# A third weight buffer, a later second transform and piecewise adds in a fused attention and mixing kernel

## The chip, the cores and the metric

The kernel runs on one core of one Trainium2 chip. The metric is the device time of one execution in microseconds (us). The profiler also records the span, the time from the first to the last instruction of the execution; the device time is a little longer.

## What is computed

Three blocks follow each other, for 2 batches of 768 tokens:

```python
# attention: 8 heads of 64, each token sees 4 sink keys and a window of 128 keys
a = softmax(where(is_sink | in_window, q @ k.T / 8, -1e9)); x = a @ v        # (2, 768, 512)
# token mixing
theta = x @ w_theta
y = w_tok_r @ (x * cos(theta)) + w_tok_i @ (x * sin(theta))
u = x + y
x = u + relu(u @ w_ch)
# Fourier mixing and a wide layer
u = x + real(fft(fft(x, axis=1), axis=2))
un = (u - mean(u)) / sqrt(var(u) + 1e-6)
out = u + relu(un @ w_ch1) @ w_ch2        # 512 -> 2048 -> 512
```

The weights arrive as 64-bit floats and are turned into 32-bit floats on the chip.

## The kernel before

**Numbers.** A matmul operand is split into a high part and the rest (`split`: a copy on ScalarE, ACT, makes the high part, a subtraction on GpSimd, POOL, or on VectorE, DVE, makes the rest), and each product is three matmuls on TensorE, PE.

**Weights.** A weight tile of 128 x 512 comes from memory as 128 x 1024 words of 32 bits into a raw buffer (`fetch`, one DMA of 512 KB on SP's queue). `conv` makes a 32-bit tile of it: ACT scales the high words into a slot `hs` (L268), DVE shifts them into `t` (L271), ors in bits of the low words (L272), puts the sign on (L275) and so writes the result `w`. Then the raw buffer is free for the next DMA. `ahead(depth)` keeps up to DEPTH transfers under way, `pump(reserve)` converts the oldest one if enough slots are free. There are 58 tiles, in this order: 4 of `w_theta`, 18 of the token weights, 4 of `w_ch`, then 16 pairs of `w_ch1` and `w_ch2`. After the attention the raw buffers are called rawb; a trace names all those loads after one tensor, `in_w_ch_dram`. `t` lies in PSUM (`self.room`) in the token mixing of batch 0 and in chunk 0, otherwise it is `w` itself.

**Slots.** Nearly all tiles are places of 128 x 512 words, handed out by `_Slots` (`take`, `give`).

**Stages.** (1) Attention and theta, to about 170 us of the span. (2) `y_gen(0)`, the token mixing of batch 0: PE accumulates in four banks `p0` (named acc and bank) and two banks `pc`, and at the end six additions on DVE put them onto the transposed activations xT (L812, L815). (3) `y_gen(1)`, the same for batch 1, and between its matmuls the channel mixing and Fourier transform of batch 0 (`chain(0)`: `ch_gen` in 6 steps, then `dft_gen` in 20). (4) The wide layer (`mlp_gen`) in four chunks of 384 rows, each of 16 steps f of 12 matmuls into `pc` and 9 into three of the banks. Chunks 0 and 1 work on batch 0, chunks 2 and 3 on batch 1. The steps of `chain(1)`, the transform of batch 1, are put between the steps f of the wide layer, and in chunk 0 what is left of the weights is fetched and converted. For each f, `jit_split` splits the two weight tiles anew, one step ahead, on ACT (L194) and POOL (L200).

In the transform, `groups` adds and splits spectra (DVE, ACT, POOL), PE multiplies them into two tiles s of 128 x 258 and 128 x 256, ACT copies one of them to a mirror buffer `bs` (L966), GpSimd clears column 0 of `bs` (L967), and DVE makes Y of both.

The calls stand in program order, but a scheduler that works with a timeline of its own decides the final order on each engine; each engine then runs its list strictly in order.

Of the kernel before, what the change touches and what calls it, by code (L numbers as in the profile page):

```python
# [11 lines left out]
F32 = mybir.dt.float32  # L12
F32R = mybir.dt.float32r
I32 = mybir.dt.int32
AF = mybir.ActivationFunctionType
ALU = mybir.AluOpType
# [12 lines left out]
TILES = [(0, False), (3, False), (1, False), (1, True), (2, False), (2, True)]  # L29
GROUPS = [0, 3, 1, 2]  # L30
NSLOT = 67
NSLOT2 = 15
T0 = 2
DEPTH = 2
NRAW = 2
NRAW1 = 3
NJIT = 12
IL = 1
# [2 lines left out]
C1E = 12  # L41
# [29 lines left out]
C1N = 2  # L71
# [55 lines left out]
class _Slots:  # L127
# [5 lines left out]
    def grow(self, pool, n):  # L133
        self.free.extend((pool, f"s{i}") for i in range(n))

    def take(self, *shape, dt=F32, name="t"):
        place = self.free.popleft()
        t = place[0].tile([128, *shape], dt, tag=place[1], name=name, bufs=1)
        if place in self.last:
            self.pairs.append((self.last[place], t))  # L140
        self.last[place] = t
        self.own[id(t)] = (place, t, self.free)
        return t
# [35 lines left out]
class _Body:  # L179
# [76 lines left out]
    def conv(self, tile_):  # L256

        nc = self.nc
        raw = tile_.bitcast(I32)
        w = self.take(512)  # L260

        t = (self.room.next() if self.room else w).bitcast(I32)
        hs = self.take(512)
        v = raw.rearrange("p (n w) -> p n w", w=2)
        lo, hi = v[:, :, 0], v[:, :, 1]


        nc.scalar.activation(  # L268
            hs, raw.bitcast(F32).rearrange("p (n w) -> p n w", w=2)[:, :, 1], AF.Copy, scale=2.0 ** -112
        )  # L270
        nc.vector.tensor_scalar(t, hs.bitcast(I32), 3, None, op0=ALU.logical_shift_left)  # L271
        nc.vector.scalar_tensor_tensor(  # L272
            t, in0=lo, scalar=29, in1=t, op0=ALU.logical_shift_right, op1=ALU.bitwise_or
        )
        nc.vector.scalar_tensor_tensor(  # L275
            w.bitcast(I32), in0=hi, scalar=-0x80000000, in1=t, op0=ALU.bitwise_and, op1=ALU.bitwise_or
        )
        self.give(hs)
        self.raw.append(tile_)
        return w, w  # L280

# [490 lines left out]

    def y_gen(self, b):
        nc = self.nc
        p0 = [self.ps_acc.next() for _ in range(4)]
        pc = [self.ps_pc.next().rearrange("p (a m) -> p a m", a=2) for _ in range(2)]
        for j in range(NS):
            zz = self.z.pop((b, j))
            ws = [self.weight_split("tok", j, c) for c in (0, 2, 1)]
            for c, z in enumerate(zz):  # L780
                zh, zl = self.split(z, "a", "vp"[b], s=self.sz)
                self.give(z)
                (wh, wl), (ch, cl) = ws[2 * c], ws[1]
                cs = slice(256 * c, 256 * c + 256)
                first, last = j == 0 and c == 0, j == NS - 1 and c == 1
                def big(dd):
                    ds_ = slice(dd * 128, (dd + 1) * 128)
                    self.mm(p0[dd], zh[:, ds_], wh, first, False)
                    self.mm(p0[dd], zh[:, ds_], wl, False, False)
                    self.mm(p0[dd], zl[:, ds_], wh, False, last)  # L790

                def small(dd):
                    ds_ = slice(dd * 128, (dd + 1) * 128)
                    q = pc[dd // 2][:, dd % 2]
                    self.mm(q, zh[:, ds_], ch[:, cs], first and dd % 2 == 0, False)
                    self.mm(q, zh[:, ds_], cl[:, cs], False, False)
                    self.mm(q, zl[:, ds_], ch[:, cs], False, last)

                for dd in range(4):
                    big(dd)  # L800
                    small(dd)
                    if dd % 2:
                        if dd == 3:
                            self.give(zh, zl)
                            if c and b:
                                for k in range(3):
                                    self.give(*self.ws.pop(("tok", j, k)))
                        yield
        xt = self.xT[b]
        for dd in range(4):  # L810
            o = xt[:, dd, 0:512]
            nc.vector.tensor_tensor(o, p0[dd], o, op=ALU.add)  # L812
        for g in range(2):
            o = xt[:, 2 * g:2 * g + 2, 512:768]
            nc.vector.tensor_tensor(o, pc[g], o, op=ALU.add)  # L815


    def ch_gen(self, b, ring):
# [51 lines left out]
    def dft_gen(self, b, ring):  # L870
        nc = self.nc
        xt = self.xT[b]
        X = {}
        sums, difs = {}, {}
        for c in range(3):
            lo_, hi_ = xt[:, 0:2, 256 * c:256 * c + 256], xt[:, 2:4, 256 * c:256 * c + 256]
            e, o = self.take(2, 256), self.take(2, 256)
# [72 lines left out]
        for gi, r in enumerate(GROUPS):  # L950
# [4 lines left out]
            n = len(G[r])  # L955
# [8 lines left out]
                self.give(*hl)  # L964
            bs = self.bs.next()[:, 0:256]
            nc.scalar.activation(bs[:, 1:256], pb[:, 1:256], AF.Copy)  # L966
            nc.gpsimd.memset(bs[:, 0:1], 0.0)  # L967
            Y = self.Y.next()
            av = pa[:, 0:256].rearrange("p (r m) -> p m r", m=64)
            bv = bs.rearrange("p (r m) -> p m r", m=64)  # L970
# [25 lines left out]
                yield  # L996
        if b:
            self.give(*self.sd, *self.co, self.ce)

    def norm_tile(self, n):  # L1000
        nc = self.nc
# [97 lines left out]
    def all(self, banded):  # L1099
# [17 lines left out]
        with ExitStack() as ctx:  # L1117
            e = ctx.enter_context(tc.tile_pool(name="e2", bufs=1, reuse_waits="tile"))
            ps = ctx.enter_context(tc.tile_pool(name="ps", bufs=1, space=PSUM, reuse_waits="tile"))
            self.ps_acc = _Ring(ps, 3, [128, 512], F32, "acc", [self.bank])  # L1120
            self.ps_pc = _Ring(ps, 2, [128, 512], F32, "pc")
            self.ps_s = _Ring(ps, 2, [128, 512], F32, "s")
            self.bs = _Ring(e, 2, [128, 256], F32, "bs")
            self.Y = _Ring(e, 2, [128, 514], F32, "Y")
            self.raw = deque(e.tile([128, 1024], F32, name=f"rawb{k}") for k in range(NRAW))
            self.room = self.ps_s
            for _ in range(len(self.fetched)):
                key, raw = self.fetched.popleft()
                self.w[key] = self.conv(raw)
            self.raw = deque(list(self.raw)[0:NRAW])  # L1130
            self.s.grow(e, NSLOT2)
            self.rest()
# [5 lines left out]
    def rest(self):  # L1138
# [45 lines left out]
        for ch in range(4):  # L1184
            mg = self.mlp_gen(ch)
            for f in range(16):
                next(mg)
                if ch == 0 and f >= P2F:
                    self.pump(P2R)
                for _ in range(C1N if ch == 0 and f < C1E else 1):  # L1190
                    next(fill, None)
                if ch == 0 and f >= P2F:
                    self.pump(P2R)
                g = f - NRM[ch]
                if ch < 3 and g in (0, 2, 4):
                    self.norm_tile(3 * ch + 3 + g // 2)
                if ch < 3 and g in (2, 4, 6):
                    self.turn_norm(3 * ch + 3 + (g - 2) // 2, self.ps_s)
                if ch == 0:
                    self.mark(L2)  # L1200
            next(mg, None)
# [95 lines left out]
```

## Time and profile before

| | us |
|---|---|
| median of 3 runs | 656.09 |
| lowest and highest of them | 654.64, 656.84 |
| the profiled execution | 649.25 |
| its span | 647.4 |
| TensorE busy in it | 610.5 |
| granted TensorE clock, mean | 0.969 |

The profile was taken of one execution. A row gives the source line (L275), the engine, the operation and `out<-in` with buffer numbers left out. TensorE's busy time counts matmuls from issue to end, so that it holds short bubbles as well; what a stretch lacks in busy time is idle for certain. PEclk is the granted share of TensorE's clock: 1.00 is 2.4 GHz, half of it 1.2 GHz.

### The profile page before, as it was taken

The numbers are of one execution on the slowest core, as the hardware profiler recorded it, in microseconds if no ns is written. First come the engines' busy times: TensorE is split into PE (matmuls) and PEld (weight loads), VectorE is DVE, ScalarE is ACT, GpSimd is POOL, SyncE is SP. The second block draws the span as 40 slices with busy tenths as digits, with TensorE's granted clock in tenths as the row PEclk, the third lists the DMA queues.
The fourth block names the chain that finished last, engine by engine and source line by source line (L and its number), as shares of the span: only waits on it lengthen the run. The fifth ranks groups of instructions, "written<-read, shape, count | busy, mean of one in ns | idle before, by whom it ended". The sixth has DMA issues, their size and how long they took to land.

```text
span 647.4 us, 9463 instructions
## 1 busy us (share of the span) xinstructions
PE 610.5 (94%) x3446; PEld 524.2 (81%) x3446; DVE 351.8 (54%) x747; ACT 334.3 (52%) x776; POOL 296.1 (46%) x258
## 2 busy tenths in 40 slices
PE   8999999999999699977899987989999999999996
PEld 5767778778788499866699976978999999999995
DVE  5875748656588778697878874664211211121112
ACT  4667667777676542355543553667433444344331
POOL 1221112332584632413653568256566666565561
PEclk8589999999999989999999998999999999999999
DMA  7862423100023534503334410121000100010001
GB/s 247 302 192 82 132 66 89 43 0 2 20 95 93 161 97 132 162 33 98 98 98 131 137 60 1 32 67 50 0 1 0 51 2 0 1 50 0 1 2 55
DMA packets 23337, 46.61 MB, mean 72 GB/s; under 512 B 2512, under 2 KB 9552, under 8 KB 23280
## 3 DMA queue, kind: packets, MB, share of 16 engines
q1 hardware_dynamic: 22032, 43.74, 21.2%
q0 software_dynamic: 1248, 2.17, 1.3%
q8 instruction: 29, 0.48, 0.3%
q14 instruction: 28, 0.23, 0.1%
HBM read 42.75 MB, written 3.15 MB: 71 GB/s over the span
## 4 chain that ended last, share of the span: by engine, by line
PE 66%; DVE 13%; ACT 7%; DMA 7%; issue 4%; POOL 1%; SPq 0%; DVEq 0%; ACTq 0%
PE pc L210 21%; PE acc L210 16%; PE bank L210 6%; PE oa L210 5%; PE s L210 5%; PE th L210 5%; PE tp L215 4%; DMA rawb<-in_w_ch_dram 4%; PE sc L210 4%; DVE t L275 2%; ACT t L194 2%; DVE t L272 2%; DVE t L200 1%; DMA raw<-in_w_tok_iT_dram 1%; ACT t L268 1%
## 5 line engine op out<-in xcount | busy, mean ns | idle before, releaser
L200 POOL TENSOR_TENSOR t<-t 128x512 fp32r<-128x512 f32 x175 | 231.9, 1343 | 210.9 <-ACT t L194 188.5
L210 PE MATMUL pc<-t 128*128 128x384 f32 (+1 forms) x1056 | 199.8, 328 | 1.1 <-ACT t L194 0.6
L210 PEld LDWEIGHTS pc<-t 128*128 128x128 f32 x1056 | 183.9, 192 | 13.3 <-ACT t L194 1.2
L210 PE MATMUL acc<-t 128*128 128x512 f32 x648 | 180.8, 397 | 1.0 <-DVE xT L812 1.0
L194 ACT ACTIVATE t<-t 128x512 fp32r<-128x512 f32 x196 | 116.3, 625 | 94.5 <-PE acc L210 37.3
L210 PEld LDWEIGHTS acc<-t 128*128 128x128 f32 x648 | 117.3, 189 | 19.8 <-DVE xT L812 1.6
L1071 DVE SCALAR_TENSOR_TENSOR t<-pc,t 128x384 fp32r<-128x384 f32 x64 | 35.5, 555 | 150.9 <-ACT t L1070 150.8
L210 PE MATMUL bank<-t 128*128 128x512 f32 x216 | 68.2, 406 | 7.9 <-DVE xT L812 4.2
L210 PE MATMUL s<-t 128*128 128x256 f32 (+2 forms) x480 | 63.1, 283 | 10.7 <-POOL t L200 3.4
L210 PEld LDWEIGHTS s<-t 128*128 128x128 f32 x480 | 60.4, 189 | 14.4 <-POOL t L200 3.6
L1070 ACT ACTIVATE t<-pc 128x384 fp32r<-128x384 f32 x64 | 31.3, 489 | 70.8 <-PE pc L210 65.1
L268 ACT ACTIVATE t<-rawb 128x512 f32<-128x512 f32 x42 | 27.9, 672 | 54.8 <-DMA rawb<-in_w_ch_dram 45.5
L210 PEld LDWEIGHTS oa<-t 128*128 128x128 f32 x352 | 51.2, 209 | 2.5 <-issue 0.7
L210 PE MATMUL oa<-t 128*128 128x64 f32 x352 | 51.9, 276 | 0.0
L210 PEld LDWEIGHTS bank<-t 128*128 128x128 f32 x216 | 38.6, 189 | 16.4 <-ACT t L194 4.6
L746 POOL TENSOR_TENSOR t<-t 128x512 f32<-128x512 f32 x12 | 16.5, 1374 | 72.6 <-DVE t L745 35.1
L493 ACT ACTIVATE p<-sc,nb 128x272 f32<-128x272 f32 (+1 forms) x72 | 33.8, 472 | 18.8 <-DVE nb L489 18.7
L210 PE MATMUL th<-t 128*128 128x512 f32 x144 | 41.9, 417 | 1.5 <-DVE t L200 1.0
L215 PE MATMUL tp<-ident,p 128*128 128x128 f32 x176 | 39.6, 299 | 2.5 <-ACT p L493 2.2
L489 DVE CUSTOM_DVE_ANT_0 sc<-sc,m 128x272 f32<-128x272 f32 (+1 forms) x72 | 29.9, 429 | 18.2 <-PE sc L210 9.7
L210 PE MATMUL sc<-kst,t 64*128 64x272 f32 (+2 forms) x132 | 36.9, 466 | 0.0
L215 PEld LDWEIGHTS tp<-ident,p 128*128 128x128 f32 x176 | 27.0, 171 | 11.7 <-ACT p L493 3.7
(129 smaller groups left out, 683.5 us busy)
## 6 DMA issues: line engine op xcount, KB each, us to landing
rawb<-in_w_ch_dram SPq DMA_DIRECT2D x36, 512.0 KB, 3.6
kst<-in_k_dram SPq DMA_DIRECT2D x12, 256.0 KB, 3.4
t<-in_v_dram SPq DMA_DIRECT2D x12, 256.0 KB, 4.3
out_dram<-t SPq DMA_DIRECT2D x12, 256.0 KB, 2.1
t<-in_q_dram SPq DMA_DIRECT2D x11, 256.0 KB, 3.7
raw<-in_w_theta_dram SPq DMA_DIRECT2D x4, 512.0 KB, 6.4
raw<-in_w_tok_rT_dram SPq DMA_DIRECT2D x4, 512.0 KB, 3.8
raw<-in_w_tok_iT_dram SPq DMA_DIRECT2D x4, 512.0 KB, 4.3
```

The source lines that it names most:

```text
L194: nc.scalar.activation(o, i, AF.Copy)
L200: e.tensor_tensor(o, x, hi.bitcast(F32), op=ALU.subtract)
L210: i = self.nc.tensor.matmul(o, lhsT=lhsT, rhs=rhs, start=start, stop=stop, skip_group_check=True).ins
L215: self.chained(self.nc.tensor.transpose(o, x, ident).ins)
L268: nc.scalar.activation(hs, raw.bitcast(F32).rearrange("p (n w) -> p n w", w=2)[:, :, 1], AF.Copy, scale=2.0 ** -112)
L272: nc.vector.scalar_tensor_tensor(t, in0=lo, scalar=29, in1=t, op0=ALU.logical_shift_right, op1=ALU.bitwise_or)
L275: nc.vector.scalar_tensor_tensor(w.bitcast(I32), in0=hi, scalar=-0x80000000, in1=t, op0=ALU.bitwise_and, op1=ALU.bitwise_or)
L489: nc.vector.tensor_tensor_reduce(out=sc[:, 0:wd], in0=sc[:, 0:wd], in1=mask, op0=ALU.add, op1=ALU.min, scale=-0.125, scalar=3.0e38, accum_ ...
L493: self.last_exp = nc.scalar.activation(p[:, h, 0:wd], sc[:, 0:wd], AF.Exp, bias=nb[:, h:h + 1], scale=-1.0, accum_out=sm[:, h:h + 1]).ins
L746: nc.gpsimd.tensor_tensor(ph, km, ph, op=ALU.subtract)
L1070: nc.scalar.activation(hh, hp, AF.Relu)
L1071: nc.vector.scalar_tensor_tensor(hl, in0=hp, scalar=0.0, in1=hh.bitcast(F32), op0=ALU.max, op1=ALU.subtract)
```

## The change

Five things are changed at once.

1. NRAW and DEPTH go from 2 to 3: three raw buffers after the attention, and up to three transfers under way at all times (in the attention there were three buffers, but two transfers). NSLOT2 goes from 15 to 14 slots.
2. `conv` scales the high words in place in the raw buffer, and takes no slot `hs`; the shift (now L282) reads every second word there.
3. When a batch's transform is finished, its xT is cut into six more slots (`adopt`), for plain 32-bit tiles alone.
4. The additions of the token mixing follow piece by piece, each after the last matmul of its bank (now L814, L818), no longer all six after the last matmul.
5. Chunk 0 takes no step of `chain(1)` at f below 8 and one from f = 8; chunk 1 takes two at f below 8, then one. Before, chunk 0 took two steps at f below 12 and then one. Column 0 of the two mirror buffers is cleared once, when they are made.

```diff
-NSLOT2 = 15
+NSLOT2 = 14
-DEPTH = 2
-NRAW = 2
+DEPTH = 3
+NRAW = 3
...
+    def adopt(self, tile_):
+        flat = tile_.rearrange("p a s -> p (a s)")
+        self.free.extend((None, flat[:, 512 * k:512 * k + 512], id(tile_), k) for k in range(6))
...
-        place = self.free.popleft()
+        place = min((p for p in self.free if p[0] or dt == F32), key=lambda p: p[0] is not None)
+        self.free.remove(place)
...
-        hs = self.take(512)
...
-        nc.scalar.activation(
-            hs, raw.bitcast(F32).rearrange("p (n w) -> p n w", w=2)[:, :, 1], AF.Copy, scale=2.0 ** -112
-        )
-        nc.vector.tensor_scalar(t, hs.bitcast(I32), 3, None, op0=ALU.logical_shift_left)
+        hf = raw.bitcast(F32).rearrange("p (n w) -> p n w", w=2)[:, :, 1]
+        nc.scalar.activation(hf, hf, AF.Copy, scale=2.0 ** -112)
+        nc.vector.tensor_scalar(t, hi, 3, None, op0=ALU.logical_shift_left)
...
                 for dd in range(4):
                     big(dd)
+                    if last:
+                        o = xt[:, dd, 0:512]
+                        nc.vector.tensor_tensor(o, p0[dd], o, op=ALU.add)
                     small(dd)
+                    if last and dd % 2:
+                        o = xt[:, dd - 1:dd + 1, 512:768]
+                        nc.vector.tensor_tensor(o, pc[dd // 2], o, op=ALU.add)
...
-        xt = self.xT[b]
-        for dd in range(4):
-            o = xt[:, dd, 0:512]
-            nc.vector.tensor_tensor(o, p0[dd], o, op=ALU.add)
-        for g in range(2):
-            o = xt[:, 2 * g:2 * g + 2, 512:768]
-            nc.vector.tensor_tensor(o, pc[g], o, op=ALU.add)
...
-            nc.gpsimd.memset(bs[:, 0:1], 0.0)
...
+        self.s.adopt(xt)
...
+            for t in self.bs.tiles:
+                self.nc.gpsimd.memset(t[:, 0:1], 0.0)
...
-                for _ in range(C1N if ch == 0 and f < C1E else 1):
+                for _ in range((0, 1, 2, 1)[2 * ch + f // 8] if ch < 2 else 1):
                     next(fill, None)
```

The scheduler makes a new order of it on every engine. Three places follow, before and after; in the rows, names of the changed kernel carry other line numbers (L282, L283, L286 are the shift and the two ors of `conv`, L281 its scaling).

**VectorE at the end of the token mixing of batch 0.** Each conversion is a shift, an or and a last or; the additions onto xT_70 release the banks for batch 1; L764 is the product of x with a sine or cosine for batch 1. Before:

```order
L275 SCALAR_TENSOR_TENSOR t<-rawb_1579,s_1573 128x512
L272 SCALAR_TENSOR_TENSOR s_1574<-rawb_1580,s_1574 128x512
L275 SCALAR_TENSOR_TENSOR t<-rawb_1580,s_1574 128x512
L764 TENSOR_TENSOR t<-t 128x512
L271 TENSOR_SCALAR s_1573<-t 128x512
L812 TENSOR_TENSOR xT_70<-bank,xT_70 128x512
L272 SCALAR_TENSOR_TENSOR s_1573<-rawb_1579,s_1573 128x512
L764 TENSOR_TENSOR t<-t 128x512
L812 TENSOR_TENSOR xT_70<-acc_1568,xT_70 128x512
L815 TENSOR_TENSOR xT_70<-pc_1571,xT_70 128x2x256
```

After (L774 is the product, L814 and L818 are the additions):

```order
L283 SCALAR_TENSOR_TENSOR s_1560<-rawb_1568,s_1560 128x512
L286 SCALAR_TENSOR_TENSOR t<-rawb_1570,s_1561 128x512
L286 SCALAR_TENSOR_TENSOR t<-rawb_1568,s_1560 128x512
L282 TENSOR_SCALAR t<-rawb_1569 128x512
L283 SCALAR_TENSOR_TENSOR t<-rawb_1569,t 128x512
L774 TENSOR_TENSOR t<-t 128x512
L814 TENSOR_TENSOR xT_70<-bank,xT_70 128x512
L286 SCALAR_TENSOR_TENSOR t<-rawb_1569,t 128x512
L814 TENSOR_TENSOR xT_70<-acc_1555,xT_70 128x512
L818 TENSOR_TENSOR xT_70<-pc_1558,xT_70 128x2x256
L774 TENSOR_TENSOR t<-t 128x512
L814 TENSOR_TENSOR xT_70<-acc_1556,xT_70 128x512
```

Before, the first addition stood behind a product and the shift of the next conversion; now it stands behind the shift and the first or of the next conversion and a product, and three buffers take turns in these conversions, where two did.

**ScalarE in chunk 0, from the step that starts at f = 11 (before) and f = 9 (after).** L1070 and L1080 are the relu of the wide layer, one for each f; L268 and L281 open a conversion; L194 and L207 are high parts. Before:

```order
L1070 ACTIVATE t<-pc_1572 128x384
L194 ACTIVATE t<-s_1573 128x128
L1004 ACTIVATE mv_84<-st_80 128x1
L268 ACTIVATE t<-rawb_1580 128x512
L1004 ACTIVATE mv_85<-st_81 128x1
L966 ACTIVATE bs_1576<-s_1574 128x255
L268 ACTIVATE t<-rawb_1579 128x512
L194 ACTIVATE t<-t 128x512
L977 ACTIVATE Y_1578<-s_1573 128x1
L1070 ACTIVATE t<-pc_1571 128x384
L194 ACTIVATE t<-s_1574 128x128
L268 ACTIVATE t<-rawb_1580 128x512
```

After:

```order
L1080 ACTIVATE t<-pc_1559 128x384
L207 ACTIVATE t<-t 128x512 x2
L281 ACTIVATE rawb_1569<-rawb_1569 128x512
L281 ACTIVATE rawb_1570<-rawb_1570 128x512
L1080 ACTIVATE t<-pc_1558 128x384
L207 ACTIVATE t<-t 128x512 x2
L207 ACTIVATE t<-s_1560 128x128
L207 ACTIVATE t<-xT_71 128x512
L207 ACTIVATE t<-s_1560 128x128 x2
L1080 ACTIVATE t<-pc_1559 128x384
L207 ACTIVATE t<-s_1560 128x128
L281 ACTIVATE rawb_1568<-rawb_1568 128x512
```

Before, five conversions stood behind the relu of f = 11, three of them within two steps; now four stand behind that of f = 9, and the copies of the transform (L966, mv) are gone from between.

**TensorE where the transform of batch 1 multiplies its first two groups.** pc and acc, bank are the wide layer, s the transform, s<-ident transposes. Before, in chunk 0:

```order
L210 MATMUL s_1573<-t 128x258
L210 MATMUL s_1574<-t 128x256
L210 MATMUL s_1573<-t 128x258 x2
L210 MATMUL s_1574<-t 128x256 x2
L215 MATMUL s_1574<-ident,t 128x128 x4
L210 MATMUL pc_1572<-t 128x384 x12
L215 MATMUL s_1573<-ident,xT_71 128x128 x4
L210 MATMUL bank<-t 128x512 x2
L210 MATMUL acc_1568<-t 128x512 x2
L210 MATMUL acc_1569<-t 128x512 x2
L210 MATMUL s_1573<-t 128x258 x3
```

After, in chunk 1:

```order
L223 MATMUL pc_1558<-t 128x384 x12
L223 MATMUL s_1561<-t 128x258
L223 MATMUL s_1560<-t 128x256
L223 MATMUL acc_1557<-t 128x512 x2
L223 MATMUL bank<-t 128x512 x2
L223 MATMUL acc_1555<-t 128x512 x2
L223 MATMUL acc_1557<-t 128x512
L223 MATMUL bank<-t 128x512
L223 MATMUL acc_1555<-t 128x512
L223 MATMUL pc_1559<-t 128x384 x2
L223 MATMUL s_1561<-t 128x258 x2
L223 MATMUL s_1560<-t 128x256 x2
```

The matmuls of the high part and those of the rest of a group stood next to each other; now nine to eleven matmuls of the wide layer stand between them.

## Rows read from the trace of the kernel before

**Rows 1.** The page, span and busy time of TensorE and VectorE.
```profile
span 647.4 us, 9463 instructions
...
PE 610.5 (94%) x3446; PEld 524.2 (81%) x3446; DVE 351.8 (54%) x747; ACT 334.3 (52%) x776; POOL 296.1 (46%) x258
```

**Rows 2.** Stretches: busy PE, PEld, DVE, ACT, POOL, then PEclk, DMA share, GB/s.
```profile
176.00:210.00 34.00, 34.00 (x197) 29.82 (x196) 29.18 (x37) 23.23 (x41) 21.99 (x17) 1.00 0.31 96
210.00:224.00 14.00, 8.64 (x49) 6.96 (x47) 10.46 (x12) 8.10 (x14) 9.58 (x10) 1.00 0.60 190
224.00:240.00 16.00, 15.03 (x77) 12.94 (x78) 13.09 (x21) 7.63 (x14) 5.96 (x5) 0.79 0.30 96
...
260.00:340.00 80.00, 69.81 (x445) 61.39 (x444) 63.99 (x110) 37.62 (x83) 34.83 (x38) 1.00 0.33 96
...
382.00:440.00 58.00, 49.19 (x255) 43.48 (x254) 34.12 (x69) 34.32 (x85) 34.19 (x33) 0.94 0.09 28
...
460.00:510.00 50.00, 50.00 (x254) 45.34 (x253) 8.14 (x17) 21.20 (x43) 32.54 (x27) 1.00 0.00 1
```

**Rows 3.** Waits of TensorE, 160 to 320 us: us in total, times, longest.
```profile
PE bank L210 <- DVE xT L812: 4.2, 1, 4.2
PE s L210 <- DVE t L908: 2.5, 1, 2.5
```

**Rows 4.** The chain that ended last, 205 to 232 us: start, us, what.
```profile
218.27 3.54 DMA rawb<-in_w_ch_dram
...
221.82 0.67 ACT t L268
...
223.12 0.68 DVE xT L812
```

**Rows 5.** Timeline of VectorE, 218 to 227 us.
```profile
224.32 1.12 DVE L764 TENSOR_TENSOR t<-t 128x512 f32<-128x512 f32 x1
```

**Rows 6.** The chain that ended last, 252 to 322 us.
```profile
254.41 4.32 DMA rawb<-in_w_ch_dram
...
269.63 3.62 DMA rawb<-in_w_ch_dram
...
307.14 3.59 DMA rawb<-in_w_ch_dram
```

**Rows 7.** Waits of ScalarE, 200 to 330 us.
```profile
ACT t L268 <- DMA rawb<-in_w_ch_dram: 27.3, 14, 5.9
```

**Rows 8.** Instructions on the raw buffers rawb: time from issue to landing.
```profile
DMA to landing us min/median/max: 2.7/3.6/5.4
```

**Rows 9.** Waits of TensorE, 380 to 460 us.
```profile
PE s L210 <- POOL t L200: 3.4, 1, 3.4
```

**Rows 10.** Timeline of GpSimd, 380 to 392 us.
```profile
384.83 7.39 POOL L200 TENSOR_TENSOR t<-t 128x512 fp32r<-128x512 f32 x5 [1.46 <-ACT t L194]
```

**Rows 11.** The chain that ended last, 380 to 446 us.
```profile
421.35 3.66 DMA rawb<-in_w_ch_dram
...
425.52 4.30 DMA rawb<-in_w_ch_dram
```

**Rows 12.** Groups of VectorE by form: busy us, mean ns of one, idle before.
```profile
L1071 DVE SCALAR_TENSOR_TENSOR t<-pc,t 128x384 fp32r<-128x384 f32 x64 | 35.5, 555 | 150.9 <-ACT t L1070 150.8
...
L271 DVE TENSOR_SCALAR t<-t 128x512 int32<-128x512 int32 x27 | 13.0, 484 | 22.7 <-ACT t L268 20.7 <-ACT t L1008 1.8
...
L271 DVE TENSOR_SCALAR acc<-t 128x512 int32<-128x512 int32 x18 | 12.4, 689 | 8.3 <-ACT t L268 8.3
...
L272 DVE SCALAR_TENSOR_TENSOR t<-rawb,t 128x512 int32<-128x512 int32 x13 | 11.7, 900 | 0.1
```

**Rows 13.** Groups of ScalarE by form.
```profile
L268 ACT ACTIVATE t<-rawb 128x512 f32<-128x512 f32 x42 | 27.9, 672 | 54.8 <-DMA rawb<-in_w_ch_dram 45.5 <-PE s L210 4.1 <-DMA rawb<-in_w_tok_rT_dram 2.4
```

**Rows 14.** The line that clears column 0: duration min/median/max, first and last start.
```profile
L967 POOL MEMSET bs<- x8: 88/99/117, 181.5 to 402.9; 128x1 f32 x8
```

**Rows 15.** The page, the group of subtractions on GpSimd.
```profile
L200 POOL TENSOR_TENSOR t<-t 128x512 fp32r<-128x512 f32 x175 | 231.9, 1343 | 210.9 <-ACT t L194 188.5
```

More of the change, by code (lines that the diff above doesn't have):

```diff
@@ L134, in grow @@
         self.free.extend((pool, f"s{i}") for i in range(n))
+    def adopt(self, tile_):
+        flat = tile_.rearrange("p a s -> p (a s)")
+        self.free.extend((None, flat[:, 512 * k:512 * k + 512], id(tile_), k) for k in range(6))
     def take(self, *shape, dt=F32, name="t"):
-        place = self.free.popleft()
+        place = min((p for p in self.free if p[0] or dt == F32), key=lambda p: p[0] is not None)
+        self.free.remove(place)
+        if place[0] is None:
+            n = int(np.prod(shape))
+            t = place[1][:, 0:n]
+            if len(shape) > 1:
+                t = t.rearrange("p (a b) -> p a b", a=shape[0])
+            self.own[id(t)] = (place, t, self.free)
+            return t
         t = place[0].tile([128, *shape], dt, tag=place[1], name=name, bufs=1)
@@ L277, in conv @@
         )
-        self.give(hs)
         self.raw.append(tile_)
@@ L774, in y_gen @@
         nc = self.nc
+        xt = self.xT[b]
         p0 = [self.ps_acc.next() for _ in range(4)]
```

## The prediction, made before the result was known

> **What bounds the kernel now.** I read the page first, then a table of stretches, then the waits and the chain in the stretches that lack something. The page [rows 1] says that TensorE is busy 610.5 of 647.4 us, VectorE 351.8: TensorE is the bound on average, and no matmul is added or removed. So only time in which TensorE stands or runs slowly can be won. The stretches [rows 2] show where that is. At 176 to 210 and 460 to 510 us busy time fills the stretch. Three places lack some:
>
> - End of batch 0's token mixing: 210 to 240 us lacks 14 - 8.64 = 5.4 and 16 - 15.03 = 1.0, and runs 16 us at a granted share of 0.79, which loses 16 x 0.21 = 3.4. Together 9.7.
> - Batch 1's token mixing with batch 0's transform, up to the start of the wide layer: 80 - 69.81 = 10.2 in 260 to 340.
> - The second half of chunk 0: 58 - 49.19 = 8.8, and 58 x 0.06 = 3.5 at a share of 0.94. Together 12.3.
>
> That is 32 us that the change could touch; the attention ahead of it has its own losses, which it leaves.
>
> **The first place.** TensorE waits 4.2 us there for the first addition onto xT [rows 3]. The chain [rows 4] says why that addition is late: a raw buffer comes free, its DMA takes 3.54 us, ACT scales it at 221.82, the shift follows on VectorE, and only then, at 223.12, the addition, because it stands behind that shift in VectorE's order. What is late is a weight that nobody needs yet. Two edits act on it. With three buffers a DMA may be issued one conversion earlier. One conversion is three operations of some 0.69 us [rows 12], so about 2.1 us of VectorE; two conversions now lie between a buffer's release and its next use, 4.1 us against a landing of 3.6 [rows 8]. The wait of VectorE on a landing is gone or under 1 us. And the additions may start after the last matmul of their bank: 21 matmuls of the last piece follow the first of them, 3.6 us at the 34 us for 197 of [rows 2]. What stays: in the new order the additions are still mixed with the last or of a conversion (0.69) and a product (1.12, [rows 5]), and VectorE arrives with 10.46 of 14 us of work in 210 to 224 [rows 2], so it may reach the first addition late. If it starts just when TensorE runs out, the second and third bank come free 0.69 + 0.68 = 1.4 and 0.68 + 1.12 + 0.68 = 2.5 us later (0.68 an addition, [rows 4]) against 0.6 us of matmuls for each bank (three at 50 us for 254), and TensorE loses 0.8 + 1.9 = 2.7 us. If it is on time it loses nothing. I take the late case and no slow clock behind such short stops, so this term is 9.7 - 2.7 = 7. Bounds: 0 (VectorE as late as before, the clock falls as before) and 9.7.
>
> **The second place.** The chain through 252 to 322 us holds three landings of 4.32, 3.62 and 3.59 us [rows 6], and ACT waits for landings 27.3 us in 14 pieces [rows 7]. Behind each such wait stand copies of the transform on ACT, then sums on VectorE; TensorE's 2.5 us stop there is for a sum, L908 [rows 3]. A third buffer moves these landings ahead by a conversion. But between the landings the chain runs on VectorE, busy 64 of the 80 us [rows 2], and that work stays. In the new order 28 tiles are at least begun before this stretch and 15 are left for it, where 24 were and 17 are: 2 x 2.1 = 4 us less on VectorE. I take 4 of the 10.2 us as won; bounds 0 (VectorE's own work fills the gaps) and 8 (all but the start of chunk 0).
>
> **The third place.** Two things stop TensorE in chunk 0. At 386 us it waits 3.4 us for GpSimd [rows 9], which works through five subtractions in 7.39 us [rows 10]: the rest part of a group's spectrum, wanted right behind the high part. And at 421 and 425 us the chain holds two landings of 3.66 and 4.30 us [rows 11] for the weights of f = 13 and 14, just in time. In the new order nine to eleven matmuls of the wide layer, some 2 us, stand between high part and rest, against one subtraction of 1.34 [rows 15]. The last four conversions start behind the relu of f = 9 and not of f = 11; 18 of 32 weight tiles are done before chunk 0 instead of 15, because `hs` is no longer taken and six slots of xT come in. Is there a new load? In f = 1 to 6 of the new chunk 0 stand 10 conversions, 1.67 a step. A step has 21 matmuls, 4.1 us at 50 us for 254 [rows 2], and five smaller ones of the channel mixing, up to 0.9. VectorE has 1.67 x 2.07 + 0.56 = 4.0 us in it [rows 12], ACT 1.67 scalings, two high parts and a relu, at 0.67 each at most [rows 13] 3.1, GpSimd 2 x 1.34 = 2.7 [rows 15], and each of three buffers turns once in 3 / 1.67 x 4.7 = 8.4 us, which holds a landing and a conversion. All are below TensorE. In chunk 1 the group stage has 4 x 2.7 + 6 x 1.34 = 18.8 us on GpSimd in four steps, against 4 x 4.1 and 36 matmuls of the transform (up to 6.2 us) on TensorE, 22 us: full but not over. I take 9 of the 12.3 as won; bounds -6 (the stops move to chunk 1, and it has a slow clock too) and 12.
>
> **The rest.** The scaling in place reads and now also writes with a step of two words. 0.67 us [rows 13] is with the strided read. No row has a strided write; if it doubled that, the 15 conversions of the second place brought 15 x 0.67 = 10 us onto ACT, which has 42 of 80 us free there [rows 2]. I take nothing. The shift now reads with a step of two words. Into PSUM it already takes 0.69 us [rows 12]. Into SBUF it takes 0.48, and an or that reads the raw buffer 0.90; between 0.69 and 0.90 lies its price with a stride, if the stride has one. 26 tiles are shifted so, 14 in the attention and 12 in the second place, so 12 x 0.2 to 0.4 = 2.5 to 5 us on VectorE there. TensorE is not stopped by VectorE all the time; I leave this inside the second place, whose 4 is below the middle of what its three landings cost.
>
> Here the Trainium skill is of two minds, in "VectorE: DVE Perf Modes": its section on mode 1x has unusual strides fall back to one element a cycle, its section on mode 2x_2P asks only for SBUF and an even dimension. By the first, the shift loses its double rate, and if all of it lay on the path the sum below would be 16.5; by the second it loses nothing and the sum stands. No row of before has this shift with a stride.
>
> Clearing column 0 takes 0.1 us eight times on GpSimd [rows 14]; six of them go: under 0.6 us, hidden. In the attention 17 tiles are converted instead of 14, 3 x 2.1 us on VectorE and 3 loads more on SP's queue, each behind the release of its buffer and ahead of loads of q and v. TensorE is nearly full there; I charge 1 us, bounds -3 and 1.
>
> **Sum.** 7 + 4 + 9 - 1 = 19 us. The profiled execution took 649.25 us, so 630. It lies 6.8 us below the median of the three runs shown, 656.09; the same gain off the median gives 637.
>
> **Rivals.**
>
> - *VectorE holds the second place and the first.* For it: 64 of 80 us busy, and the chain between the landings is VectorE's. Against it: the chain needs the landings as well, and 4 us of work leave. Then the first place gives 4, the second 0, the third 5, the attention -1: 8 won, 648.
> - *The transform stops chunk 1 (slower than before).* Chunk 0 has marks that keep the scheduler from running ahead; chunk 1 has none. Each of the 16 steps taken in its first eight f ends in ACT, VectorE or GpSimd, and TensorE's order is fixed. If half of these 16 cost the 3.4 us of [rows 9], 27 us are lost; from six such stops on (20 us) the 19 us won are eaten. With eight the time is 656 - 19 + 27 = 664. Against it: in the new order matmuls of the wide layer stand between all parts of a group, and beside the wide layer alone VectorE has 8, ACT 21 and GpSimd 32.5 us of work in 50 [rows 2].
> - *The third buffer changes nothing*, as VectorE sets the pace everywhere: the first place wins 4, the attention loses 1 and the strided shift 2.5 on the path; 655 to 657. Against it: four of the waits of [rows 4, 6] are landings.
>
> **Chances.** The forecast (624 to 645) 0.64; VectorE as the limit (645 to 653) 0.18; no change 0.07; slower 0.11. A difference of 0.3%, 2 us, is about what a measurement of this kernel can tell from none. Faster is 0.82, same 0.07, slower 0.11. Two in ten are left out by a range from 626 (all upper bounds give 29 us, which leaves 627) to 653 (the rival where VectorE holds). The likeliest case alone has 628 to 645.
>
> **What would show it.** Right: the wait for the first addition under 2 us and a full granted share behind it; ACT's wait for landings well under half; no landing in the chain in the second half of chunk 0; the group stage in chunk 1 with under 1 us of wait for GpSimd. Wrong: waits for s in 400 to 470 us, landings of over 5 us with three under way, VectorE over 90% in 226 to 320, or a longer attention.

## The result, and the profile after

The changed kernel takes 637.77 us (median of 4 runs, 632.27 to 639.56); the kernel before, run beside it, takes 655.37 us (4 runs, 653.67 to 656.84). The ratio is 0.9718, 95% interval 0.965 to 0.9786. The forecast was 637.0, range 626 to 653.

The profiled execution of the changed kernel took 639.56 us. Its page, to be held against [rows 1]:

```profile
span 637.8 us, 9444 instructions
...
PE 611.9 (96%) x3446; PEld 524.3 (82%) x3446; DVE 351.7 (55%) x747; ACT 334.1 (52%) x776; POOL 299.2 (47%) x252
```

Each engine has about the work that it had. TensorE's share rises from 94 to 96%: what went is idle time, 36.9 us before (647.4 - 610.5), 25.9 now (637.8 - 611.9). The stretches, with the columns of [rows 2]:

```profile
175.00:210.00 35.00, 35.00 (x204) 30.68 (x203) 32.66 (x42) 27.52 (x48) 24.65 (x19) 1.00 0.30 98
210.00:240.00 30.00, 25.13 (x131) 21.53 (x131) 27.03 (x42) 17.61 (x32) 15.82 (x13) 0.89 0.50 155
...
373.00:416.00 43.00, 41.80 (x252) 38.51 (x251) 29.49 (x43) 17.90 (x38) 25.13 (x19) 1.00 0.05 13
416.00:458.00 42.00, 41.72 (x238) 38.30 (x238) 21.03 (x31) 21.93 (x43) 28.58 (x22) 1.00 0.05 20
458.00:501.00 43.00, 43.00 (x244) 39.59 (x243) 16.54 (x42) 24.51 (x66) 26.32 (x30) 1.00 0.05 19
```

The last three are the second half of chunk 0 and the two halves of chunk 1, which now carries the transform: together 1.5 us idle in 128, at the full clock. The third place is gone. The stretch 210 to 240 is nearly as bad as it was: 4.87 us idle, and 3.3 us lost at 0.89 of the clock, 8.2 together against 9.7 before. TensorE's waits from 160 to 320 us (columns as in [rows 3]) name the same first line, with the same length:

```profile
PE bank L223 <- DVE xT L814: 4.2, 1, 4.2
PE s L228 <- DVE st L1001: 3.1, 1, 3.1
```

ScalarE's waits from 200 to 330 us, which were 27.3 us in 14 pieces in [rows 7]:

```profile
ACT rawb L281 <- DMA rawb<-in_w_ch_dram: 10.5, 8, 4.1
```

From 240 to 320 us the chain that ended last holds no landing, where [rows 6] has three between 252 and 322; the only one up to 335 is this, after batch 1's mixing:

```profile
320.55 3.67 DMA rawb<-in_w_ch_dram
```

To see where the time went, each profiled execution is cut at four starts, found in its timeline: the first token-mixing matmul (into pc), the first addition onto xT, the first 128x384 matmul of the wide layer, the relu of chunk 2's first step. (In brackets: how many us of the attention ran at half clock.) The stretch up to the wide layer holds the same 560 matmuls in every run but e9, where it holds 579.

| kernel profiled | attention | to first addition | to wide layer | to chunk 2 | rest |
|---|---|---|---|---|---|
| before | 169.8 (23.9) | 53.3 | 98.6 | 188.0 | 137.6 |
| before, again (e5) | 176.8 (34.1) | 54.0 | 100.4 | 188.4 | 137.7 |
| changed | 175.4 (27.3) | 52.2 | 93.3 | 180.4 | 136.5 |
| e1 additions at the end | 175.5 (34.1) | 52.0 | 93.1 | 181.9 | 136.6 |
| e2 steps as before | 171.5 (17.1) | 52.2 | 92.5 | 180.5 | 138.0 |
| e3 two buffers | 179.9 (36.7) | 52.8 | 100.8 | 183.0 | 136.8 |
| e4 two loads in attention | 184.8 (33.7) | 54.4 | 89.5 | 180.0 | 136.5 |
| e6 attention as before | 172.1 (23.9) | 55.6 | 91.4 | 179.7 | 136.1 |
| e7 pending tiles early | 170.8 (17.1) | 51.3 | 92.1 | 179.8 | 136.2 |
| e8 scaling into a slot | 169.6 (17.1) | 55.8 | 94.7 | 178.3 | 136.2 |
| e9 additions ahead | 173.6 (27.3) | 45.7 | 107.8 | 180.0 | 137.3 |
| e10 as e7, again | 174.0 (30.7) | 50.7 | 92.2 | 179.7 | 136.1 |

Against the first line, the changed kernel wins 1.1, 5.3, 7.6 and 1.1 us behind the attention, 15.1 in all, and 18.1 against the second line. The last 1.1 us belong to the 7.6: 649 matmuls stand behind the start of chunk 2 in the changed kernel, 660 before, so that 11 of them now stand ahead of it. The attention's length differs by 7 us between two executions of one and the same kernel.

### The profile page after: what moved, and what is told of

It is laid out like the page before. It is cut to its first block, busy times and chain, and to the rows that moved or that the text cites. A ratio compares the mean times of both kernels' runs of the same rounds, so it can differ in the third digit from the quotient of the medians.

```text
span 637.8 us, 9444 instructions
## 1 busy us (share of the span) xinstructions
PE 611.9 (96%) x3446; PEld 524.3 (82%) x3446; DVE 351.7 (55%) x747; ACT 334.1 (52%) x776; POOL 299.2 (47%) x252
## 4 chain that ended last, share of the span: by engine, by line
PE 80%; DVE 9%; DMA 3%; ACT 3%; issue 3%; SPq 0%; DVEq 0%; ACTq 0%
PE pc L223 23%; PE acc L223 19%; PE s L223 9%; PE bank L223 8%; PE oa L223 5%; PE th L223 5%; PE sc L223 4%; PE tp L228 4%; DVE t L286 2%; PE s L228 1%; DMA rawb<-in_w_ch_dram 1%; DMA raw<-in_w_tok_iT_dram 1%; DMA rawb<-in_w_tok_rT_dram 1%; DVE t L213 1%; PE bank L382 1%
## 5 line engine op out<-in xcount | busy, mean ns | idle before, releaser
L213 POOL TENSOR_TENSOR t<-t 128x512 fp32r<-128x512 f32 x151 | 202.6, 1360 | 197.9 <-ACT t L207 163.7
L223 PE MATMUL acc<-t 128*128 128x512 f32 x648 | 180.4, 398 | 1.1 <-DVE xT L814 0.7
L207 ACT ACTIVATE t<-t 128x512 fp32r<-128x512 f32 x172 | 102.0, 625 | 102.3 <-PE acc L223 32.5
L223 PE MATMUL bank<-t 128*128 128x512 f32 x216 | 65.9, 402 | 5.4 <-DVE xT L814 4.2
L213 POOL TENSOR_TENSOR t<-xT,t 128x512 fp32r<-128x512 f32 x39 | 51.1, 1325 | 33.3 <-ACT xT L740 18.6
L223 PE MATMUL s<-t 128*128 128x256 f32 (+2 forms) x480 | 66.5, 286 | 0.2 <-DVE st L1001 0.2
L223 PEld LDWEIGHTS s<-t 128*128 128x128 f32 x480 | 63.6, 194 | 2.5 <-DVE st L1001 1.0
L1080 ACT ACTIVATE t<-pc 128x384 fp32r<-128x384 f32 x64 | 31.3, 488 | 63.9 <-PE pc L223 62.4
L223 PE MATMUL oa<-t 128*128 128x64 f32 x352 | 50.4, 269 | 0.0
L223 PE MATMUL th<-t 128*128 128x512 f32 x144 | 44.8, 438 | 2.3 <-ACT t L207 1.2
L281 ACT ACTIVATE rawb<-rawb 128x512 f32<-128x512 f32 x41 | 27.6, 676 | 23.3 <-DMA rawb<-in_w_ch_dram 18.8
```

The lines of the kernel that those rows point to most:

```text
L207: nc.scalar.activation(o, i, AF.Copy)
L213: e.tensor_tensor(o, x, hi.bitcast(F32), op=ALU.subtract)
L223: i = self.nc.tensor.matmul(o, lhsT=lhsT, rhs=rhs, start=start, stop=stop, skip_group_check=True).ins
L281: nc.scalar.activation(hf, hf, AF.Copy, scale=2.0 ** -112)
L1080: nc.scalar.activation(hh, hp, AF.Relu)
```

## The experiments

Each kernel differs from the changed one by the edit shown, unless it says otherwise. Two theories stood against each other. One: the transfers bind, and the third buffer brings the gain. The other: the new table of steps (edit 5) brings it, by pulling the transform's parts apart.

**e1: the additions at the end again.**

```diff
-                    if last:
-                        o = xt[:, dd, 0:512]
-                        nc.vector.tensor_tensor(o, p0[dd], o, op=ALU.add)
...
+        for dd in range(4):
+            o = xt[:, dd, 0:512]
+            nc.vector.tensor_tensor(o, p0[dd], o, op=ALU.add)
...
```

> The changed kernel with the six additions written after the last matmul again (edit 4 undone). The order of the attention with window, instruction by instruction on all five engines, comes out the same as that of the changed kernel, so this is also a second look at it. If the piecewise additions are worth something: 638 + up to 7 = 645 us. If the scheduler had placed them so anyway: 638 us, a ratio to before of 0.972, and TensorE again waits about 4 us for the first addition; what differs from the changed kernel's profile is then the spread of one execution.

It took 636.58 us (6 runs, 633.80 to 640.89), ratio 0.9741 (0.9701 to 0.9781): as the changed kernel. The order of the instructions is the same on all five engines with this edit and without it; the scheduler had already put the additions there. Edit 4 is worth nothing.

**e2: the steps of batch 1's transform as before.**

```diff
-                for _ in range((0, 1, 2, 1)[2 * ch + f // 8] if ch < 2 else 1):
+                for _ in range(C1N if ch == 0 and f < C1E else 1):
```

> The changed kernel with the old table of steps: chunk 0 takes two steps of the transform of batch 1 at each f below 12 (edit 5 undone); third buffer, slots and scaling in place stay. Theory S, the gain comes from moving the transform into chunk 1: 638 + 13 = 651 us, ratio 0.993, TensorE stops again in chunk 0. Theory B, the gain comes from earlier weights (buffer and slots): 638 to 640 us, ratio 0.973 to 0.976.

638.08 us (6 runs, 636.82 to 642.04), ratio 0.9797 (0.9754 to 0.984). Up to chunk 2 the profile has 180.5 us, the changed one 180.4: with three buffers the old table wins the third place too. Only the rest is 1.5 us longer, 138.0, and it holds the 11 matmuls more that it held before; behind the attention the two kernels differ by 0.8 us (463.2 and 462.4). TensorE's waits from 372 to 500 us, where [rows 9] had 3.4 for GpSimd, hold none for it:

```profile
PE s L223 <- DVE st L1001: 1.7, 1, 1.7
PE s L228 <- ACT bs L976: 0.6, 1, 0.6
PE bank L223 <- ACT t L1080: 0.5, 1, 0.5
PE s L223 <- ACT bs L976: 0.5, 1, 0.5
```

**e3: two buffers and two loads, the rest as changed.**

```diff
-NSLOT2 = 14
+NSLOT2 = 15
...
-DEPTH = 3
-NRAW = 3
+DEPTH = 2
+NRAW = 2
```

> The changed kernel with NRAW = 2, DEPTH = 2 and NSLOT2 = 15 again; table of steps, scaling in place and the slots of xT stay. Theory S: 638 to 642 us; the loads at the start of the token mixing are issued at some 176 us and not at 190. Theory B: 650 to 655 us, with landings of weights on the chain again.

652.63 us (12 runs, 650.01 to 655.21), ratio 1.0005 (0.9978 to 1.0031): the gain is gone. ScalarE waits for landings as in [rows 7], from 200 to 330 us:

```profile
ACT rawb L281 <- DMA rawb<-in_w_ch_dram: 30.7, 14, 5.1
```

and the chain from 235 to 440 us holds ten landings, of which the first four lie in the second place:

```profile
245.32 3.72 DMA rawb<-in_w_ch_dram
251.79 3.62 DMA rawb<-in_w_ch_dram
261.41 3.55 DMA rawb<-in_w_ch_dram
280.87 4.48 DMA rawb<-in_w_ch_dram
...
374.45 3.63 DMA rawb<-in_w_ch_dram
```

The second place is back at 100.8 us. The third is not: 183.0, 5 us below before. So buffer and table reach the third place by two roads that overlap: with two buffers the new table, the slots and the scaling win 5 us of it, with the old table the buffer, the slots and the scaling win 7.5, and all together 7.6. That the whole of e3 stays level means that its attention is some 4 us longer in the median than before's. Worked out as the median, less the 2 us outside the span, less what lies behind the attention: 652.63 - 1.9 - 473.4 = 177.3, against 652.91 (the kernel before in 17 runs beside it) - 1.9 - 480.5 = 170.5, or with 477.5 in place of 480.5, 173.5. Part of it shows in the trace. Two loads under way with the scaling in place give the attention of e3 and e4 another order than the changed kernel's, the same in both, and there TensorE stands 4.7 us from 60 us on (1.4 in the changed kernel), with a half clock of 3.4 us that begins shortly before the end. So e3 takes back more than the third buffer gave behind the attention, which is 473.4 - 462.4 = 11 us.

**e4: two loads under way in the attention, three after it.** The first place was as bad as before; perhaps the loads ahead of it start too late (189.78 us, against 175.67 before).

```diff
+        depth = depth or self.depth
...
+        self.depth = 2
...
+            self.depth = DEPTH
```

> The changed kernel with at most two transfers under way in the attention, and three after it. In the changed kernel a third tile waits to be converted when the attention ends; its last operation runs at 189 us, and the first load into the new buffers is issued at 189.8, against 175.7 before. If this lateness eats what the third buffer wins in the token mixing of batch 0: loads from about 176 us on, a wait for the first addition under 2 us, 638 - 5 = 633 us. Rival, VectorE and the landings set the pace there with any start: 637 to 640 us and a wait of about 4 us.

644.89 us (6 runs, 640.92 to 649.94), ratio 0.9882 (0.9833 to 0.993). The attention costs 184.8 us in the profile: besides the stops named under e3, TensorE stands 10.3 us in its first 60 us, against 6.4 in the changed kernel, for a reason not looked into. The first load is issued at 190.9 us, no earlier than in the changed kernel, so that this run says nothing about late loads; the wait for the first addition grows to 6.5 us.

**e5: the kernel before, unchanged, a second profile.**

> The kernel before, profiled a second time. Its first profile took 649.25 us, where its median is 653 to 655. If that profile had a quick attention by luck of the clock: the token mixing now starts at 173 to 176 us and not at 169.8, and the stages behind it last as they did (53, 99 and 188 us, within 1 us). Rival, the stages behind differ too: then single profiles can't be set against each other by stage.

One execution, 659.16 us, more than any of the 11 runs beside it (650.87 to 657.75). Behind the attention every stretch lies within 2 us of the first profile (1.8 the most, where 1 was expected), the attention is 7.0 us longer. Both views are of 0 to 60 us; first the first profile of before, then this one, columns as in [rows 2]:

```profile
0.00:60.00 60.00, 56.22 (x277) 40.16 (x279) 39.92 (x138) 36.00 (x109) 11.84 (x14) 0.80 0.67 222
```

```profile
0.00:60.00 60.00, 53.51 (x228) 37.33 (x229) 37.64 (x128) 32.38 (x97) 11.85 (x14) 0.72 0.63 207
```

The granted share is 0.80 in one and 0.72 in the other, and 49 matmuls fewer are done by 60 us. Over the attention, 10.2 us more at half clock (34.1 and 23.9) cost 5.1 us, and TensorE stands 2.7 us more in these 60 us (56.22 and 53.51 busy).

**e6: the attention of before** (its `hs` and two loads under way there, the changed kernel behind it).

```diff
+        hs = self.take(512) if self.depth == 2 else None
+        ho = hs if hs is not None else hf
+        nc.scalar.activation(ho, hf, AF.Copy, scale=2.0 ** -112)
...
+        self.depth = 2
...
+            self.depth = DEPTH
```

> The changed kernel with the old conversion (a slot hs) and two transfers under way in the attention, the new ones behind it. On all engines its order is that of the kernel before through the attention. If the changed attention costs 3 to 5 us by its three more conversions: 637 - 4 = 633 us. Rival, the attention differs by the clock alone: 637 us. A gain over 8 us in the token mixing of batch 0 would say that the tile left over at the attention's end was the trouble there.

636.51 us (6 runs, 634.34 to 643.19), ratio 0.9749 (0.97 to 0.9797): as the changed kernel. The first loads start at 177.9 us, 12 us earlier than in the changed kernel, and the wait for the first addition is still 6.4 us. The late loads are not the cause.

**e7: the tiles left over from the attention are converted before `room` is set**, so that their `t` is the result itself and not a bank of PSUM that frees later.

```diff
-            self.room = self.ps_s
             for _ in range(len(self.fetched)):
                 key, raw = self.fetched.popleft()
                 self.w[key] = self.conv(raw)
+            self.room = self.ps_s
```

> The changed kernel, but the three tiles under way at the end of the attention are converted without a PSUM bank for their middle step, so that VectorE need not wait for banks of the attention. If the late loads (189.8 us) cost the first place its gain: first load at about 176 us, wait for the first addition under 2 us, 637 - 5 = 632 us. Rival, VectorE is full there (32.7 of 35 us): first addition as late as before, 637 us.

633.39 us (6 runs, 631.99 to 635.9), ratio 0.9697 (0.9661 to 0.9733). The loads start at 157.1 us, 33 us earlier than in the changed kernel, and the wait is still there:

```profile
PE bank L223 <- DVE xT L814: 3.6, 1, 3.6
```

**e8: the scaling into a slot again** (edit 2 undone, the rest as changed).

```diff
-        nc.scalar.activation(hf, hf, AF.Copy, scale=2.0 ** -112)
-        nc.vector.tensor_scalar(t, hi, 3, None, op0=ALU.logical_shift_left)
+        hs = self.take(512)
+        ho = hs if hs is not None else hf
+        nc.scalar.activation(ho, hf, AF.Copy, scale=2.0 ** -112)
...
+            t, hi if hs is None else hs.bitcast(I32), 3, None, op0=ALU.logical_shift_left
...
```

> The changed kernel with the scaled high words in a slot hs again (edit 2 undone), third buffer, table and slots of xT kept. If the slot matters: fewer tiles are converted before chunk 0 and the time goes up by 3 to 6 us, 640 to 643. If the shift's double rate matters more: the shift into SBUF takes 0.48 us again and the time falls by up to 3 us, 634. If neither: 637 us within 2.

637.79 us (6 runs, 634.98 to 639.93), ratio 0.9754 (0.9715 to 0.9793): neither gain nor loss from edit 2.

**e9: no conversion between the last matmuls and the additions.** It starts from e7: `pump` stops at the 18th piece of `y_gen(0)`, and conversions of the next six pieces may stand at most 10 matmuls ahead.

```diff
-            if u in P3S:
+            if u in P3S and n < 18:
...
+        self.lag = 10
         for n, _ in enumerate(self.y_gen(1)):
+            if n == 6:
+                self.lag = 100
```

> Starts from the kernel with the pending tiles early. In the last six pieces of batch 0's token mixing no conversion is called, and those of the first six pieces of batch 1's may not be moved ahead of the last matmuls of batch 0: 22 conversions stand ahead of the first addition onto xT instead of 28, and none of the last ones before it waits for a landing there. If conversions and their landings hold the first place, the wait for the first addition falls from 3.6 us to under 1 us and the 3.4 to 6.8 us at half clock behind it go; the stretch from the first product with y to the first addition is 48 to 50 us instead of 51.3. The six conversions (6 x 2.1 = 12 us of VectorE) then come in the stretch up to the wide layer. If VectorE's work sets that stretch, it gives the gain back there (95 to 98 us instead of 92.1) and the whole stays at 631 to 636; if not, the whole is 626 to 630. Rival: the addition is late for another reason (the product of 1.12 us ahead of it, slow subtractions); then the wait stays above 3 us.

644.12 us (6 runs, 640.66 to 646.14), ratio 0.9838 (0.9794 to 0.9882), and **e10**, which is e7 once more beside it:

> The kernel with the pending tiles early once more, as the measure for the run beside it: 631 to 636 us, a wait for the first addition of 3 to 4 us, 51 to 53 us from the first product with y to the first addition and 91 to 93 us up to the wide layer. Rival: its 633.39 came of a quick attention, and the time is that of the changed kernel, 636 to 639.

635.22 us (6 runs, 632.84 to 641.04), ratio 0.9744 (0.9689 to 0.98). In e9 the wait for the addition is gone from TensorE's list of 150 to 330 us, which begins now:

```profile
PE s L223 <- ACT t L207: 6.2, 2, 4.6
PE s L228 <- DVE st L1002: 3.0, 1, 3.0
```

The first place is won, 45.7 us against 50.7, and no half clock follows it at once. But the second place takes 107.8 us instead of 92.2 (95 to 98 were expected at worst), and the kernel is 9 us slower than e10. The stretches up to the first addition and from there to the wide layer, of e9:

```profile
174.00:219.00 45.00, 44.82 (x256) 38.70 (x256) 39.83 (x39) 30.45 (x54) 27.60 (x21) 1.00 0.23 74
219.00:327.00 108.00, 94.86 (x582) 84.60 (x582) 87.01 (x135) 45.94 (x94) 41.95 (x37) 0.94 0.33 98
```

and of e10:

```profile
174.00:224.00 50.00, 48.47 (x280) 42.36 (x278) 47.28 (x57) 36.79 (x64) 36.30 (x26) 1.00 0.37 111
224.00:317.00 93.00, 88.19 (x561) 79.66 (x562) 70.50 (x119) 39.80 (x83) 33.33 (x33) 0.94 0.29 90
```

VectorE has 87.0 us to do in the second stretch instead of 70.5. The six conversions (12.4 us at 2.07) are most of these 16.5 us, and the stretch grows by 15.6. But VectorE's work is not all that came back. With three buffers ScalarE waits for landings again, from 200 to 330 us (11.3 us in e10):

```profile
ACT rawb L281 <- DMA rawb<-in_w_ch_dram: 25.3, 7, 8.1
```

and the chain from 219 to 327 us holds three of them:

```profile
255.61 4.35 DMA rawb<-in_w_ch_dram
...
264.76 3.72 DMA rawb<-in_w_ch_dram
...
272.30 6.46 DMA rawb<-in_w_ch_dram
```

## Why the prediction was right in the sum, and where it was not

**The first place, 7 us: mis-sized, it gave 1.1.** The step that failed is "I take the late case and no slow clock behind such short stops": VectorE was to start the first addition just when TensorE runs out, TensorE was to lose 2.7 us, and the clock nothing. In the changed kernel TensorE's last matmul ahead of it ends at 224.2 us and the addition starts at 227.53, 3.3 us later (3.4 before). TensorE stands 4.87 us, and the 6.8 us at half clock behind the stop, 3.4 us of the forecast's 9.7, stayed with it.

The premise, "The wait of VectorE on a landing is gone or under 1 us", nearly came true. From 175 to 228 us VectorE has three such waits, 1.0 us the longest (columns as in [rows 3]):

```profile
DVE s L282 <- ACT rawb L281: 1.9, 3, 1.0
```

The longest stands in the chain from 205 to 240 us:

```profile
217.91 4.24 DMA rawb<-in_w_ch_dram
...
222.17 0.67 ACT rawb L281
...
222.86 0.69 DVE s L282
...
227.61 0.60 DVE xT L814
```

For this landing of 4.24 us and the scaling behind it VectorE stood only 1.0 us, from 221.84 on, and behind that it works almost without a gap up to the addition, 4.8 us (222.86 to 227.61). Without this wait and the one of 0.6 us before it the addition would still come some 1.7 us after TensorE ran out (an estimate, 3.3 - 1.6). What makes it late is work. 28 conversions are begun ahead of the addition where 24 were. The prediction read that from the order and credited the second place with two of the four; it charged none to the first place, where they are some 8 us: VectorE is busy 48.4 of the 52.2 us up to the addition, 44.1 of 53.3 before. e9 shows both sides: with 22 conversions ahead the wait goes, 5.0 us are won, and the second place pays 15.6.

**The second place, 4 us: right in size, it gave 5.3, and the cause is shown in part.** Landings left the chain, ScalarE's wait for them fell to 38% (10.5 of 27.3), and e3 shows that the third buffer does it: with two, 100.8 us. How it does it is open, for two things go together. In the changed kernel 12 conversions (counted by their first or) stand between the first addition and the wide layer; before there are 16, in e3 17, in e9 18. The runs with 11 or 12 take 89.5 to 94.7 us, those with 16 to 18 take 98.6 to 107.8, and in e9 the landings are back on the chain in spite of three buffers. So the buffer helps this stretch at least in part by letting four conversions run ahead of it; what it hides of the landings themselves was not tried apart. That VectorE's own work sets what is left, as the text held, is true of one stop. 88% of the chain from 240 to 320 us is now TensorE's own work. What remains is its wait of 3.1 us for a sum, and ahead of it the chain runs over VectorE's conversions:

```profile
300.07 0.43 DVE t L282
...
304.72 1.47 DVE t L286
306.19 0.60 DVE t L1001
```

**The third place, 9 us: 7.6, or 8.7 with the 1.1 us behind chunk 2's start, right in size, half wrong in cause.** Both stops are gone, as [rows 9, 11] would have it. But that the wait for GpSimd goes because the wide layer's matmuls now stand between high part and rest is refuted: in e2 TensorE's order at these groups is row for row that of before, and no such wait is left. What changed is GpSimd's order: before, TensorE's matmul at 389.78 us was released by the third of the subtractions of [rows 10], which ended at 389.73; in e2 it starts at 380.87 us, released by the first of a like row, which started at 379.33 and ended at 380.81. Nor is the table needed while there are three buffers. Which of the new slots, the freed `hs`, the table and the earlier conversions wins the 5 us that e3 keeps was not tried apart. A lead in tiles at the chunk's start is not needed to win this place: at the first relu of the wide layer 41 conversions are done before, 43 in the changed kernel, and 40 in e2. In the changed kernel's chunk 0 the chain now ends its second half in the transform's sums on VectorE and not in a landing:

```profile
401.64 1.78 DVE t L889
...
406.07 1.44 DVE t L894
```

**The rest.** The attention was charged 1 us. Its profile shows 175.4 against 169.8, but 176.8 in e5; by the median, as worked out under e3, it is 637.77 - 1.8 - 462.4 = 173.6, against 173.0 to 176.0 (655.37 - 1.9, less 480.5 or 477.5). No loss can be told from none. Its count was off: by the traces 17 tiles go through the attention's buffers where 16 did, not 14; 14 of them are converted before the token mixing starts, in both kernels. The 1.1 us behind chunk 2's start, which no term held, come with the table and its 11 matmuls: e2 has 138.0 there.

The scaling in place and the shift with a stride, priced at nothing and at up to 0.2 to 0.4 us each, cost nothing that the runs show (e8). By form, in the changed kernel (busy us, mean ns):

```profile
L282 DVE TENSOR_SCALAR t<-raw 128x512 int32<-128x512 int32 x14 | 7.2, 519 | 5.2 <-ACT raw L281 5.1
...
L282 DVE TENSOR_SCALAR t<-rawb 128x512 int32<-128x512 int32 x12 | 5.1, 431 | 4.1 <-PE s L223 1.6 <-PE acc L223 1.4 <-ACT rawb L281 1.1
```

```profile
L281 ACT ACTIVATE rawb<-rawb 128x512 f32<-128x512 f32 x41 | 27.6, 676 | 23.3 <-DMA rawb<-in_w_ch_dram 18.8 <-DMA rawb<-in_w_tok_iT_dram 4.2
```

431 and 519 ns with the stride, 484 without it in [rows 12] (the medians are 418 and 426 against 426); 676 ns for the scaling, 672 in [rows 13]. The Trainium skill, "VectorE: DVE Perf Modes", section on mode 2x_2P, asks only for SBUF and an even dimension, and the shift agrees with it. The section on mode 1x lists unusual strides among what that mode takes; for this stride no fall to it shows. What would have decided it ahead is another page of the Trainium skill, "SBUF — State Buffer", section "Door 1: The DMA port swizzle": accesses keep their rate as long as two of them fall on one line of 16 bytes, which a step of two 32-bit words still does. Both durations agree with it.

**The rivals.** That VectorE holds the second place is half right: the stop that remains there is for its work, but 5.3 us were won, where this rival gave 0. The transform stops nothing in chunk 1 (0.28 and 0.00 us idle in its halves). That the third buffer changes nothing is excluded by e3. Of the marks set, ScalarE's wait, the third place's chain and the group stage came as forecast; the wait for the first addition and the clock behind it did not. Of the marks for wrong one came: two landings took 5.97 and 6.81 us, both among the first loads at 190 us, where TensorE did not stop. Behind the attention the forecast had 20 us. Held against the first profile of before, the terms missed by -5.9 (first place), +1.3 (second) and -0.3 (third, with the 1.1 us behind it), which leaves 15.1; against the second profile it is 18.1; and the attention's 1 us was not lost. The medians' gain of 17.6 lies between: that the sum came out so close is in part luck, for the first place missed by 5.9 us, a third of the gain, and the spread between profiles of one kernel, 3 us behind the attention and 7 in it, is of the size of that miss. It is no proof of the parts.

**A better version?** e7 was measured twice, at 0.9697 and 0.9744 of before, the changed kernel at 0.9718. It starts the loads 33 us earlier, and no run tells it from the changed kernel.

## What to carry to other kernels

Here a third buffer paid in the stretches whose chain held landings (11 us behind the attention between e3 and the changed kernel), and about 1 us in the one where VectorE, which converts, had 44.1 of 53.3 us to do and got four conversions more: read the chain and the busy time of each stretch, not the average. Work that a scheduler moves forward is a credit in the stretch that it leaves and a debit in the one that it enters; book it on both, above all where the engine is as full as VectorE was here (48.4 of 52.2 us). Before an edit that moves instructions in the source is priced, see whether the final order moves at all: here the additions did not. And an edit undone for a test can change the order elsewhere: e3 also got a slower attention, so that its ratio of 1.0005 is more than the buffer.

## What was not expected of the hardware

The granted clock of the first 60 us differs between executions of the same kernel, 0.80 and 0.72 for the kernel before. Its attention was 7.0 us longer in the second, of which the clock explains 5.1 us (10.2 us more at half clock); a single profile's attention can't be compared with another's without it. At the first place a stop of 3.0 to 6.5 us goes with 6.8 us at half clock in all eleven profiles that have the stop (the half clock starts at 224.5 us in the kernel before and at 229.3 in the changed one); e9 has neither. A shift that reads every second word of SBUF keeps the rate that it has without a stride (431 and 519 ns against 484).
